# Seven block products for the outputs of six systems in the last pass of layer two, and squared Relu as two ScalarE steps

## The chip, the cores and the metric

The kernel runs on one core of one Trainium2 chip (trn2). The metric is device microseconds of one execution. A profiled execution gives busy times per engine and a trace of every instruction: PE is TensorE's matmul, PEld its weight load, DVE VectorE, ACT ScalarE, POOL GpSimd, SP the engine that issues the DMAs. The mean granted clock of TensorE over the span is 1.000, its level of 2.4 GHz.

## What is computed

A retention attention feeds two feed-forward layers on 2304 tokens of 512 features. The change lies in the second layer, which is, cut to what matters:

```python
def _moe2_ref(x, w_in, w_out):       # x [2304, 512], w_in [512, 2048], w_out [2048, 512]
    h = x @ w_in
    r = np.maximum(h, 0.0)
    g = r * r                        # squared Relu
    return (g @ w_out).astype(np.float32)
```

All values are float32. The kernel multiplies in a fast float32 form (F32R). Each operand is split into a high part and a low part (`hi`, and `lo` = value minus `hi`), and a product is the three matmuls hi by hi, hi by lo and lo by hi.

## The kernel before

Layer two runs in three passes `(2, 0)`, `(2, 1)`, `(2, 2)` of 768 tokens, each of two halves "a" and "b" of 384. A pass has eight **systems** `k` = 0 to 7. A system is 256 of the 2048 hidden features for the pass's 768 tokens, and its `x @ w_in` is computed with seven block products where a plain two-by-two block multiplication has eight (a Strassen-Winograd scheme). So a system has seven **slots** (function `slot`), each of six matmuls of 384 columns (function `product`). A slot accumulates in a PSUM bank (names g, v and z in the trace), and ACT and DVE read the bank between slots: slots 1, 6, 7 and 4 follow each other on one bank, and ACT's copy of one slot must be over before the next may write.

Slots 2, 4 and 3 finish the hidden values (`cag` for half "a", `cbg` for "b"). Squared Relu is there one DVE instruction on `max(x, 0) * x`; in slot 4 ACT does the Relu first. Then `hidden` makes the `hi` part with a cast on ACT and the `lo` part with a subtraction on DVE, 768 columns each (`ho_hi`, `ho_lo`).

The output product is function `out2`. After every second system, the pair's 512 hidden features are multiplied by 512 rows of `w_out`, in six tiles of 128 tokens by 512 features. A tile is twelve matmuls of 512 columns in one of three PSUM banks (`oacc`), and DVE adds it into `xy` (ACT copies it there for the first pair). `xy` holds the layer's input and takes its output. The very last tile is done in two halves of 256 columns. The operands of `w_out` lie split in DRAM (`wsp`), those of `w_in` as sums and splits in `win`; SP loads both a system ahead (`wi`, `wo`).

The program is not run in the order in which it is written: a scheduler takes the code's order as priority and puts an instruction in its engine's queue when its inputs are expected to be there. Each engine then works through its queue in order. So what stands behind what on an engine is fixed when the kernel is built, and a tile of a pool is written again only when its last reader is through. The dictionary `outs` says in which system's loop the tiles of a pair are written out in code, and the loop over `n` at the end writes, for each system, its slots, its loads and those tiles.

Of the kernel before, what the change touches and what calls it, by code (L numbers as in the profile page):

```python
# [12 lines left out]
U32 = mybir.dt.uint32  # L13
# [42 lines left out]

TINY = float(np.uint32(0x38000000).view(np.float32))
# [4 lines left out]
def retention_moe_kernel(  # L62
# [19 lines left out]
    raw_p = pool(ctx, "raw_p", 2)  # L82
    cv_p = pool(ctx, "cv_p", 3)
    mid = ExitStack()
    ctx.enter_context(mid)
    cv2_p = pool(mid, "cv2_p", HOLD - 2)
# [291 lines left out]
    s1_p = pool(ctx, "s1_p", 1, side="right")  # L378
    xs_p = pool(ctx, "xs_p", 4, side="right")
    xo_p = pool(ctx, "xo_p", 1, side="right")  # L380

# [231 lines left out]
    c4_p = pool(ctx, "c4_p", 1, side="right")  # L613
# [34 lines left out]

    def slot(n, i):
# [5 lines left out]
        if i == 1:  # L655
# [9 lines left out]
        relu2 = dict(scalar=0.0, op0=ALU.max, op1=ALU.mult)  # L665
# [10 lines left out]
        elif i == 2:  # L676
            tt(out=a[:, 0], in0=s["z"], in1=a[:, 0], op=ALU.add)
            if what == "g":
                act.activation(out=a[:, 0], in_=a[:, 0], **silu)
            elif what == "v":  # L680
                tt(out=ga[:, 0], in0=a[:, 0], in1=ga[:, 0], op=ALU.mult)
            else:
                dve.scalar_tensor_tensor(out=a[:, 0], in0=a[:, 0], in1=a[:, 0], **relu2)
        elif i == 4:
            if what == "g":
                act.activation(out=a[:, 1], in_=x, **silu)
            elif what == "v":
                tt(out=ga[:, 1], in0=x, in1=ga[:, 1], op=ALU.mult)
                hidden(n, "a", ga)
            else:  # L690
                act.activation(out=a[:, 1], in_=x, func=AF.Relu)
                dve.scalar_tensor_tensor(out=a[:, 1], in0=x, in1=a[:, 1], **relu2)
                hidden(n, "a", a)
        elif i == 3:
# [7 lines left out]
            else:  # L702
                dve.scalar_tensor_tensor(out=b, in0=b, in1=b, **relu2)
# [5 lines left out]
    def hidden(n, which, c):  # L709
        kw = dict(bufs=2) if n > flip - 1 and which == "a" else {}  # L710
# [51 lines left out]
    def out2(n, which, j):  # L762
# [3 lines left out]
        final = n == len(systems) - 1 and which == "b" and j == 2  # L766
        for at in (slice(0, 256), slice(256, 512)) if final else (slice(0, 512),):
            o = out_bank()[:, at]
            for r in range(4):
                w = wos[2 * k - 2 + r]  # L770
                h = [x[:, r % 2, j * P:(j + 1) * P] for x in hid[n - 1 + r // 2, which]]
                three(o, h, (w[:, 0, at], w[:, 1, at]), r == 0, r == 3)
            home = xy[:, at.start // P:at.stop // P, t0:t0 + P]
            src = o.rearrange("p (c q) -> p c q", q=P)
            if k == 1:
                act.copy(home, src)
            else:
                tt(out=home, in0=src, in1=home, op=ALU.add)
            if k == F2 // 2 - 1:
                sp.dma_start(out=out[t0:t0 + P, at].rearrange("p (c q) -> p c q", q=P), in_=home)  # L780

    flip = systems.index((2, 0, 0, "i"))
    outs, fetch = {}, {}
    for n, (ph, p, k, what) in enumerate(systems):
# [6 lines left out]
        if what == "i":  # L791
            fetch.setdefault((n + 1 + (k + p == 0), 0), []).append((n, range(2 * k, 2 * k + 2)))
        if what == "i" and k % 2:
            for x, which in enumerate("ab"):
                outs.setdefault(n + 2 + x, []).extend((out2, n, which, j) for j in range(3))
# [19 lines left out]
    for n in range(end + 4):  # L815
# [24 lines left out]
        for x in fetch.get((n, 0), []):  # L840
            load_out(*x)
        for x in seq:
# [7 lines left out]
            if n == flip + 1 and i == 4:  # L850
# [3 lines left out]
                ho_p = pool(ctx, "ho2_p", 3)  # L854
                wo_p = pool(ctx, "wo2_p", 8)
# [7 lines left out]
            place[:] = place[1:] + [dve.recent]  # L863
            if (ph, p) in PACE:
# [5 lines left out]
        for _ in make:  # L870
            pass
        if (ph, p) == (2, 0) and systems[n + 1][1]:
            for _ in convert:
                pass

# [60 lines left out]
```

## Time and profile before

| what | value |
|---|---|
| three runs | 875.12, 876.67, 877.28 us, median 876.67 us |
| span of the profiled execution | 875.1 us |
| PE, PEld busy | 863.9 us (99%), 746.0 us (85%) |
| DVE, ACT, POOL busy | 642.8 us (73%), 400.9 us (46%), 122.2 us (14%) |
| matmuls | 5064 |
| DMA | 203.62 MB, 233 GB/s over the span |

The profiled execution's span agrees with the lowest of the three runs to a tenth of a microsecond, so next to nothing lies around it; the median is 1.5 us above it. Matmuls overlap in PE's pipeline: the duration of one is longer than the step to the next, so the pace is read from start to start. A row of the timeline that says "x2" holds two instructions.

### The profile page before, as it was taken

Reading aid. Unit: us, or ns where it says so; the run is one execution under the profiler, and the core shown is the slowest. Engines: PE = TensorE matmul, PEld = TensorE weight load, DVE = VectorE, ACT = ScalarE, POOL = GpSimd, SP = SyncE. Lnnn points to the kernel's source line nnn. Section 1 sums busy time; section 2 is a strip of 40 time slices with the busy share of each in tenths; the row PEclk is TensorE's granted clock in tenths of the full one; section 3 lists DMA queues with packets and bytes.
Section 4 is the critical chain, followed back from the end, with each engine's and each line's share of the span. In section 5 each row is a group of like instructions: output and inputs, shape, how many; then the busy total and the mean of one; then the engine's idle time right before and its main releaser. Section 6 shows DMA issues by size and latency. Waiting matters only on the chain.

```text
span 875.1 us, 13516 instructions
## 1 busy us (share of the span) xinstructions
PE 863.9 (99%) x5064; PEld 746.0 (85%) x5064; DVE 642.8 (73%) x1002; ACT 400.9 (46%) x709; POOL 122.2 (14%) x135
## 2 busy tenths in 40 slices
PE   9989999999999999999999999999999999999998
PEld 7878888888888888888888899989899988998987
DVE  3899999998976899677647999999534467533544
ACT  3657777565544544644325466554233233232310
POOL 3343343223130010000002311120000000000000
PEclk9999999999999999999999999999999999999999
DMA  9994777755554489878745388988666465656412
GB/s 337 402 356 160 253 249 249 264 186 211 196 192 154 139 282 379 297 273 288 253 141 185 144 315 328 361 304 313 206 239 215 126 226 210 190 202 204 164 41 73
DMA packets 75218, 203.62 MB, mean 233 GB/s; under 512 B 7696, under 2 KB 18448, under 8 KB 75152
## 3 DMA queue, kind: packets, MB, share of 16 engines
q1 hardware_dynamic: 74720, 202.34, 65.8%
q8 instruction: 40, 0.66, 0.3%
q10 hardware_dynamic: 432, 0.41, 0.1%
q14 instruction: 26, 0.21, 0.1%
HBM read 138.23 MB, written 64.49 MB: 232 GB/s over the span
## 4 chain that ended last, share of the span: by engine, by line
PE 86%; DVE 7%; DMA 4%; issue 2%; ACT 1%; SPq 0%; POOL 0%; DVEq 0%; POOLq 0%; ACTq 0%
PE oacc L113 42%; PE g L113 24%; PE v L113 12%; PE z L113 6%; DVE w L113 3%; DMA qk_sb<-in_qk 3%; DVE wi L113 1%; PE o L113 1%; DMA k_sb<-in_kv 1%; DMA qs_sb<-in_qscale 1%; PE s L113 1%; DVE xy L113 1%; DVE cbg L113 0%; PE kv L113 0%; DVE xo_l L113 0%
## 5 line engine op out<-in xcount | busy, mean ns | idle before, releaser
L113 PE MATMUL g<-xo_h,wi 128*128 128x384 f32 (+1 forms) x768 | 238.3, 364 | 0.0
L113 PE MATMUL oacc<-wo,ho_hi 128*128 128x512 f32 (+1 forms) x584 | 179.5, 388 | 0.0
L113 PEld LDWEIGHTS g<-xo_h,wi 128*128 128x128 f32 x768 | 142.5, 188 | 17.1
L113 PE MATMUL oacc<-ho_hi,wo 128*128 128x512 f32 (+1 forms) x480 | 151.1, 370 | 0.5 <-ACT xy L113 0.5
L113 DVE TENSOR_TENSOR xy<-oacc,xy 128x512 f32<-128x512 f32 (+1 forms) x155 | 99.6, 648 | 59.6 <-PE oacc L113 59.1
L113 PE MATMUL g<-xo_l,wi 128*128 128x384 f32 (+1 forms) x384 | 139.6, 364 | 0.0
L113 PEld LDWEIGHTS oacc<-wo,ho_hi 128*128 128x128 f32 x584 | 108.4, 188 | 19.2
L113 PE MATMUL v<-xo_h,wi 128*128 128x512 f32 (+1 forms) x384 | 123.2, 364 | 0.0
L113 PE MATMUL oacc<-wo,ho_lo 128*128 128x512 f32 (+1 forms) x292 | 113.3, 390 | 0.0
L113 PEld LDWEIGHTS oacc<-ho_hi,wo 128*128 128x128 f32 x480 | 88.1, 188 | 17.6 <-ACT xy L113 1.3
L113 PE MATMUL oacc<-ho_lo,wo 128*128 128x512 f32 (+1 forms) x240 | 89.1, 371 | 0.0
L113 PEld LDWEIGHTS g<-xo_l,wi 128*128 128x128 f32 x384 | 72.1, 188 | 8.4
L113 DVE TENSOR_SCALAR w<-w 128x512 f32<-128x512 f32 (+1 forms) x136 | 64.9, 480 | 18.0 <-ACT w L113 17.0
L113 PEld LDWEIGHTS v<-xo_h,wi 128*128 128x128 f32 x384 | 71.2, 188 | 8.0
L113 DVE TENSOR_TENSOR cbg<-v,cbg 128x384 f32<-128x384 f32 (+1 forms) x72 | 43.1, 598 | 45.8 <-ACT cbg L113 24.3
L113 ACT ACTIVATE cag<-g 128x384 f32<-128x384 f32 (+1 forms) x36 | 19.0, 528 | 125.2 <-PE g L113 125.1
L113 PE MATMUL v<-xo_l,wi 128*128 128x512 f32 (+1 forms) x192 | 69.8, 363 | 0.0
L113 PEld LDWEIGHTS oacc<-wo,ho_lo 128*128 128x128 f32 x292 | 54.8, 188 | 11.2
L113 PE MATMUL z<-xo_h,wi 128*128 128x512 f32 (+1 forms) x192 | 62.5, 365 | 0.0
L113 ACT CAST ho_hi<-cbg 128x768 fp32r<-128x768 f32 (+1 forms) x36 | 32.7, 908 | 45.5 <-DVE cbg L113 44.4
L113 DVE SCALAR_TENSOR_TENSOR w<-raw,w 128x512 uint32<-128x512 uint32 x68 | 52.5, 773 | 0.7
L113 PEld LDWEIGHTS oacc<-ho_lo,wo 128*128 128x128 f32 x240 | 45.1, 188 | 8.7
(90 smaller groups left out, 1295.6 us busy)
## 6 DMA issues: line engine op xcount, KB each, us to landing
wi<-win SPq DMA_DIRECT2D x84, 512.0 KB, 4.2
raw<-in_w SPq DMA_DIRECT2D x68, 512.0 KB, 4.9
win<-wi SPq DMA_DIRECT2D x60, 512.0 KB, 3.6
wo<-wsp SPq DMA_DIRECT2D x44, 512.0 KB, 6.4
wsp<-wo SPq DMA_DIRECT2D x28, 512.0 KB, 5.2
qk_sb<-in_qk SPq DMA_DIRECT2D x15, 576.0 KB, 7.4
wst<-w SPq DMA_DIRECT2D x32, 256.0 KB, 6.0
wi<-win SPq DMA_DIRECT2D x28, 256.0 KB, 5.4
```

What stands on the lines that cost most here:

```text
L113: i = op(*args, **kw)
```

## The change

Three things change in layer two.

**Squared Relu.** Function `square` does it as Relu and then Square, both on ACT, for all 24 systems. DVE's three instructions per system go.

**Seven products for the outputs.** For systems 0 to 5 of the last pass (`turn_over` is its first system, `PAIRED` = 6) the output of a pair and of 128 tokens of each half is a two-by-two block product with seven products: block rows are 128 tokens of "a" and 128 of "b", block columns 256 output features, and the inner blocks are the pair's 256 features by 256. Function `out3` does one product: six matmuls of 256 columns, in one half of a bank. The bank is not started afresh for each: products 6, 7 and 4 go on top of product 1, product 3 on top of 5, and each state of the bank is added into one or two of `xy`'s blocks before the next product is put on top. For the first pair ACT copies four of the seven. The left operands are three blocks and four sums of blocks of the hidden values. GpSimd makes the sums (`sums2`, four instructions for each 128 tokens, in the part of `xy` that earlier passes have already written out), and `prepare` splits blocks and sums: ACT casts 512, 256 and 1024 columns, DVE subtracts as many (`hs_h`, `hs_l`, two buffers in pool `hl_p`). The hidden values lie in tiles of a pair (`caa`, `cab`), in two pools that take turns. Systems 6 and 7 keep the plain product (`whole`, `out4`).

**Operands of `w_out`.** The four sums of blocks are made during pass `(2, 1)` (`operand_sums`: GpSimd sums, ACT casts and DVE subtractions of 256 columns) and stored in DRAM (`tsp`). In the last pass each system's seven operands are loaded one by one (256 KB each, tile `wt`, functions `operands2` and `follow`). A list `stream` holds the 63 products and the six last tiles; `flow` takes 1.5 of them, later 2.2, with each slot, from the 26th slot of the last loop on, and what is left after the last slot.

```diff
+PRODUCTS = (1, 5, 6, 3, 7, 2, 4)
+SUMS = (6, 5, 4, 7)
+PAIRED = 6
+START = 4
+    def square(dst, src):
+        act.activation(out=dst, in_=src, func=AF.Relu)
+        act.activation(out=dst, in_=dst, func=AF.Square)
...
-                dve.scalar_tensor_tensor(out=a[:, 0], in0=a[:, 0], in1=a[:, 0], **relu2)
+                square(a[:, 0], a[:, 0])
...
-                act.activation(out=a[:, 1], in_=x, func=AF.Relu)
-                dve.scalar_tensor_tensor(out=a[:, 1], in0=x, in1=a[:, 1], **relu2)
+                square(a[:, 1], x)
...
-                dve.scalar_tensor_tensor(out=b, in0=b, in1=b, **relu2)
+                square(b, b)
...
     def hidden(n, which, c):
+        if n >= turn_over:
+            return
...
+    def sums2(n, j):
+        a, b = (x[:, :, :, j * P:(j + 1) * P] for x in pairs_of[n])
+        a11, a12, a21, a22 = (x[:, :, f] for x in (a, b) for f in range(2))
+        sums_of[n, j] = s = xy[:, :, 2 * P * j:2 * P * (j + 1)].rearrange("p i (s q) -> p i s q", q=P)
+        for x, y, z, op in ((0, a21, a22, ALU.add), (2, a11, a21, ALU.subtract),
+                            (1, s[:, 0], a11, ALU.subtract), (3, a12, s[:, 1], ALU.subtract)):
+            pool_e.tensor_tensor(out=s[:, x], in0=y, in1=z, op=op)
+    def prepare(n, j):
+        a, b = (x[:, :, :, j * P:(j + 1) * P] for x in pairs_of[n])
+        hi, lo = (hl_p.tile([P, 7, 2, P], F32R, tag=x, name=f"hs_{x}") for x in "hl")
+        halves[n, j] = hi, lo
+        split(hi[:, 0:2], lo[:, 0:2], a.rearrange("p s f q -> p f s q"))
+        split(hi[:, 2], lo[:, 2], b[:, :, 1])
+        split(hi[:, 3:7], lo[:, 3:7], sums_of[n, j])
+    def out3(n, j, at):
+        ph, p, k, what = systems[n]
+        i = PRODUCTS[at]
+        if at < 2:
+            bank_ = (2, 1 + j % 2 * 2)[at == 0]
+            banks[at] = ps_a.tile([P, 512], F32, tag=f"a{bank_}", name="oacc")
+        o = banks[at % 2 if at < 6 else 0]
+        o = o[:, 256:] if i == 2 else o[:, :256]
+        x = (1, 2, 4, 5, 6, 7, 3).index(i)
+        for s in range(2):
+            hi, lo = (z[:, x, s] for z in halves[n, j])
+            th, tl = (moving[n - 1 + s, i][:, y] for y in range(2))
+            for y, (c, d) in enumerate(((hi, th), (hi, tl), (lo, th))):
+                pe.matmul(
+                    o, c, d, start=i in (1, 5, 2) and s + y == 0, stop=s == 1 and y == 2, skip_group_check=True
+                )
+        which, half = {1: (0, 0), 5: (1, 1), 6: (0, 1), 3: (0, 1), 7: (1, 1), 2: (0, 0), 4: (1, 0)}[i]
...
+        if k == 1 and i in (1, 5, 6, 4):
+            act.copy(home, src)
+        else:
+            tt(out=home, in0=src, in1=home, op=ALU.add)
...
+    def ready_halves():
+        while queue and prepared["n"] < flowed["out"] + 2:
+            n, j = queue.pop(0)
+            (whole if n == end - 1 else prepare)(n, j)
+            prepared["n"] += 1
...
+            past = slots["n"] - begin_at
+            flow(min(int(1.5 * past + 0.7 * max(0, past - 28)), 21 * PAIRED // 2))
```

How this moves the queues is shown at three places; in the rows, names carry their buffer numbers.

**TensorE behind its last slots.** Before, when the slots of the last system are through, a tile of twelve matmuls of 512 columns follows another (three banks, here `oacc_8278`, `oacc_8293`):

```order
L113 MATMUL oacc_8264<-wo_7972,ho_lo_8063 128x512
L113 MATMUL oacc_8278<-wo_8089,ho_hi_8170 128x512 x2
L113 MATMUL oacc_8278<-wo_8089,ho_lo_8171 128x512
L113 MATMUL oacc_8278<-wo_8091,ho_hi_8170 128x512 x2
L113 MATMUL oacc_8278<-wo_8091,ho_lo_8171 128x512
L113 MATMUL oacc_8293<-wo_8089,ho_hi_8170 128x512 x2
L113 MATMUL oacc_8293<-wo_8089,ho_lo_8171 128x512
L113 MATMUL oacc_8293<-wo_8091,ho_hi_8170 128x512 x2
L113 MATMUL oacc_8293<-wo_8091,ho_lo_8171 128x512
```

Now there are two stretches of block products with no slot between them. The first holds 14; it begins with the end of the first pair (`oacc_8145`, halves `hs_h_7990`), and then products of the second pair's first block of tokens (`hs_h_8115`, banks `oacc_8255` and `oacc_8274`) and of its second block (`hs_h_8238`, bank `oacc_8364`) take turns:

```order
L122 MATMUL oacc_8145<-wt_7627,hs_h_7990 128x256 x2
L122 MATMUL oacc_8145<-wt_7627,hs_l_7991 128x256
L122 MATMUL oacc_8255<-wt_7913,hs_h_8115 128x256 x2
L122 MATMUL oacc_8255<-wt_7913,hs_l_8116 128x256
L122 MATMUL oacc_8255<-wt_8131,hs_h_8115 128x256 x2
L122 MATMUL oacc_8255<-wt_8131,hs_l_8116 128x256
L122 MATMUL oacc_8274<-wt_7937,hs_h_8115 128x256 x2
L122 MATMUL oacc_8274<-wt_7937,hs_l_8116 128x256
L122 MATMUL oacc_8274<-wt_8131,hs_h_8115 128x256 x2
L122 MATMUL oacc_8274<-wt_8131,hs_l_8116 128x256
L122 MATMUL oacc_8364<-wt_7913,hs_h_8238 128x256 x2
L122 MATMUL oacc_8364<-wt_7913,hs_l_8239 128x256
```

So three banks take turns and a bank comes back after two other products. The second stretch, behind the last slots, holds 19 and has the same form.

**VectorE beside that.** Before, the last splits and sums into `xy` lie between finished tiles:

```order
L113 SCALAR_TENSOR_TENSOR cbg_8095<-cbg_8095 128x2x384
L113 TENSOR_TENSOR ho_lo_8235<-cag_8094,ho_hi_8234 128x768
L113 TENSOR_TENSOR ho_lo_8261<-cbg_8095,ho_hi_8260 128x768
L113 TENSOR_TENSOR xy_78<-oacc_8278,xy_78 128x4x128
L113 TENSOR_TENSOR xy_78<-oacc_8293,xy_78 128x4x128
```

Now the three splits of the second block (`hs_l_8239`) stand between the sums that make the banks free:

```order
L122 TENSOR_TENSOR hs_l_8239<-caa_7753,hs_h_8238 128x512
L122 TENSOR_TENSOR xy_78<-oacc_8255,xy_78 128x2x128
L122 TENSOR_TENSOR hs_l_8239<-cab_7754,hs_h_8238 128x256
L122 TENSOR_TENSOR xy_78<-oacc_8274,xy_78 128x2x128
L122 TENSOR_TENSOR hs_l_8239<-xy_78,hs_h_8238 128x1024
L122 TENSOR_TENSOR xy_78<-oacc_8364,xy_78 128x2x128
```

Each of the two stretches has two such groups of three splits.

**GpSimd in the last pass.** Before, it has nothing to do there. Now it makes the sums, here those of the first pair (`caa_7535`, `cab_7536`), three blocks of 128 tokens one behind the other:

```order
L122 TENSOR_TENSOR xy_78<-cab_7536 128x256
L122 TENSOR_TENSOR xy_78<-caa_7535,cab_7536 128x256
L122 TENSOR_TENSOR xy_78<-cab_7536 128x256
L122 TENSOR_TENSOR xy_78<-caa_7535,cab_7536 128x256
L122 TENSOR_TENSOR xy_78<-cab_7536 128x256
L122 TENSOR_TENSOR xy_78<-caa_7535,cab_7536 128x256
L122 TENSOR_TENSOR xy_78<-xy_78,caa_7535 128x256 x3
L122 TENSOR_TENSOR xy_78<-caa_7535,xy_78 128x256 x3
```

The first block's fourth sum is the tenth of the twelve. Its cast (`hs_h_7822<-xy_78`, 1024 columns) follows on ACT, and the product that needs it stands on TensorE behind 66 matmuls of 384 columns and 12 of 256, counted from the end of the slot that completes the pair's hidden values.

## Rows read from the trace of the kernel before

**Rows 1.** Page, part 1: span; busy us (share of the span) x instructions.

```profile
span 875.1 us, 13516 instructions
PE 863.9 (99%) x5064; PEld 746.0 (85%) x5064; DVE 642.8 (73%) x1002; ACT 400.9 (46%) x709; POOL 122.2 (14%) x135
```

**Rows 2.** Waits of TensorE, whole span: waited for, us in total, times, longest.

```profile
PE s L113 <- DMA qk_sb<-in_qk: 2.6, 2, 2.2
...
PE oacc L113 <- ACT xy L113: 0.9, 3, 0.4
```

**Rows 3.** Busy us (x instructions) in two stretches of the last pass; clock, DMA share, GB/s.

```profile
760.00:820.00 60.00, 60.00 (x302) 54.13 (x301) 25.20 (x37) 17.44 (x30) 0.00 (x0) 1.00 0.58 194
820.00:875.00 55.00, 51.86 (x259) 45.52 (x257) 23.27 (x34) 8.69 (x14) 0.00 (x0) 1.00 0.27 87
```

**Rows 4.** Timeline of the end: start us, us, engine, instruction, idle before it.

```profile
867.92 0.39 PE L113 MATMUL oacc<-wo,ho_lo 128*128 128x512 f32 x1
...
868.60 0.39 PE L113 MATMUL oacc<-wo,ho_lo 128*128 128x512 f32 x1
...
869.06 0.28 PE L113 MATMUL oacc<-wo,ho_lo 128*128 128x256 f32 x1
...
871.58 0.28 PE L113 MATMUL oacc<-wo,ho_lo 128*128 128x256 f32 x1
871.90 0.42 DVE L113 TENSOR_TENSOR xy<-oacc,xy 128x256 f32<-128x256 f32 x1 [1.01 <-PE oacc L113]
```

**Rows 5.** Timeline around a wait of TensorE for the read of a bank.

```profile
134.54 0.36 ACT L113 COPY xy<-oacc 128x256 f32<-128x256 f32 x1
...
134.96 0.97 PE L113 MATMUL oacc<-xs,wb 128*128 128x256 f32 x6 [0.41 <-ACT xy L113]
...
135.77 0.88 PE L113 MATMUL oacc<-xs,wi 128*128 128x256 f32 x6
```

**Rows 6.** Timeline of TensorE, two matmuls of a slot.

```profile
702.57 0.33 PE L113 MATMUL v<-xo_l,wi 128*128 128x384 f32 x1
...
703.09 0.33 PE L113 MATMUL v<-xo_l,wi 128*128 128x384 f32 x1
```

**Rows 7.** Groups by form: busy us, mean ns of one, idle before; splits on ACT and DVE.

```profile
L113 ACT CAST wi<-w 128x512 fp32r<-128x512 f32 x36 | 22.2, 619 | 20.4 <-DVE w L113 8.8 <-POOL w L113 4.3 <-PE v L113 4.1
...
L113 ACT CAST xo_h<-xy 128x1024 fp32r<-128x1024 f32 x14 | 14.5, 1049 | 12.6 <-DVE xy L113 4.1 <-PE g L113 4.1 <-PE z L113 3.5
...
L113 DVE TENSOR_TENSOR wi<-w_in,wi 128x512 fp32r<-128x512 f32 x24 | 17.1, 716 | 2.1 <-ACT wi L113 2.1
...
L113 DVE TENSOR_TENSOR xo_l<-xy,xo_h 128x1024 fp32r<-128x1024 f32 x14 | 18.1, 1296 | 4.9 <-ACT xo_h L113 4.9
```

**Rows 8.** Groups by form: hidden values of layer two on DVE and ACT.

```profile
L113 DVE SCALAR_TENSOR_TENSOR cbg<-cbg 128x768 f32<-128x768 f32 x24 | 23.4, 974 | 0.1
...
L113 ACT CAST ho_hi<-cbg 128x768 fp32r<-128x768 f32 x24 | 20.0, 835 | 34.1 <-DVE cbg L113 33.2 <-PE oacc L113 0.8
...
L113 ACT ACTIVATE cag<-g 128x384 f32<-128x384 f32 x24 | 11.8, 493 | 102.1 <-PE g L113 102.1
...
L113 ACT ACT_TABLE_LOAD x2 | 2.6, 1283 | 2.2 <-issue 2.2
```

**Rows 9.** GpSimd on sums: one tile's min/median/max ns, then two places of its timeline.

```profile
L113 POOL TENSOR_TENSOR w_in<-w_in x16: 737/772/1492, 325.3 to 586.4; 128x256 f32<-128x256 f32 x16
...
453.43 0.74 POOL L113 TENSOR_TENSOR w_in<-s,w_in 128x256 f32<-128x256 f32 x1 [127.04 <-DVE wi L113]
454.25 0.74 POOL L113 TENSOR_TENSOR w_in<-w_in 128x256 f32<-128x256 f32 x1
...
498.11 2.57 POOL L113 TENSOR_TENSOR w_in<-s,w_in 128x256 f32<-128x256 f32 x1
```

**Rows 10.** GpSimd's same sums by form: busy us, mean ns of one, idle before.

```profile
L113 POOL TENSOR_TENSOR w_in<-w_in 128x256 f32<-128x256 f32 x16 | 14.9, 931 | 1.3
```

**Rows 11.** DMA issues: count, KB each, median us to landing.

```profile
wst<-w SPq DMA_DIRECT2D x32, 256.0 KB, 6.0
...
out<-xy SPq DMA_DIRECT2D x17, 256.0 KB, 2.7
```

More of the change, by code (lines that the diff above doesn't have):

```diff
@@ L765, in out2 @@
         t0 = TOKENS[ph, p]["ab".index(which)] + j * P
[L766 removed]
+        o = out_bank()
+        for r in range(4):
+            w = wos[2 * k - 2 + r]
+            h = [x[:, r % 2, j * P:(j + 1) * P] for x in hid[n - 1 + r // 2, which]]
+            three(o, h, (w[:, 0], w[:, 1]), r == 0, r == 3)
+        home = xy[:, :, t0:t0 + P]
+        src = o.rearrange("p (c q) -> p c q", q=P)
+        if k == 1:
+            act.copy(home, src)
+        else:
+            tt(out=home, in0=src, in1=home, op=ALU.add)
@@ new lines, in operand_sums @@
+    def operand_sums(n):
+        sums(n)
+        yield
+        yield
+        for x in range(4):
+            w = cv_p.tile([P, 512], U32, tag="w", name="tw").bitcast(F32R).rearrange("p (y q) -> p y q", y=2)
+            split(w[:, 0], w[:, 1], raw_o[n][x // 2][:, x % 2 * 256:][:, :256])
+            yield
+            soon(2, lambda x=x, w=w: sp.dma_start(out=tsp[systems[n][2]][:, x], in_=w.bitcast(F32)))
+            if x == 3 and systems[n][2] + 1 < PAIRED:
+                fetch_raw(n + 1)
@@ L814, in retention_moe_kernel @@
     end = len(systems)
-    for n in range(end + 4):
+    for n in range(turn_over):
         ph, p, k, what = systems[n] if n < end else (0, None, 0, "")
@@ L863, in retention_moe_kernel @@
             place[:] = place[1:] + [dve.recent]
+            slots["n"] += 1
+            due()
+            next(make2, None)
             if (ph, p) in PACE:
@@ L874, in retention_moe_kernel @@
                 pass
+    due(10 ** 6)
+    stream = [
+        (n, j, at) for n in range(turn_over + 1, turn_over + PAIRED, 2) for j in range(3) for at in range(7)
+    ]
+    stream += [(end - 1, j, at) for j in range(3) for at in "ab"]
+    flowed, queue, prepared = {"n": 0, "out": 0}, [], {"n": 0}
+    def ready_halves():
[3 more added lines that the diff above has]
+            prepared["n"] += 1
@@ new lines, in follow @@
+    def follow(n, j, at):
+        if at in ("a", "b"):
+            out4(n, at, j)
+        else:
+            out3(n, j, at)
+            if j == 2:
+                for m in (n + 2, n + 3):
+                    if m < turn_over + PAIRED:
+                        if at == 0:
+                            coming[m] = operands2(m)
+                            next(coming[m], None)
+                        if at % 2 or at > 3 or m % 3 != turn_over % 3:
+                            next(coming[m], None)
+        if at in (6, "b"):
+            flowed["out"] += 1
+            ready_halves()
```

194 lines of the change are left out of this document (171 added, 23 removed).

## The prediction

> **What bounds the kernel now.** I read the busy times first, then the waits, then the stretches of the last pass. TensorE is busy for 863.9 of 875.1 us, and no other engine passes 73% [rows 1]. The list of its waits ends the question of what limits layer two: all of them belong to the attention and to layer one, the largest 2.6 us, and not one to layer two [rows 2]. In the last pass TensorE fills all of 760 to 820 us while VectorE works 25.2 and ScalarE 17.4 us of the 60, GpSimd nothing, and the DMAs have 58% [rows 3]. So a microsecond of matmuls that goes is a microsecond off the time, as long as nothing else makes TensorE wait; and work taken from VectorE gives nothing by itself.
>
> **The gain.** Per pair of systems, six tiles of twelve matmuls of 512 columns become 3 x 7 products of six matmuls of 256 columns. The pace is read at the very end, where both widths run without a gap. Of 512 columns the third matmul of each row starts 0.68 us after that of the row before (867.92 to 868.60), so 0.2267 us each; of 256 columns seven such steps lie between 869.06 and 871.58, so 2.52 / 21 = 0.120 us each [rows 4]. Three pairs: 216 x 0.2267 = 49.0 us before, 378 x 0.120 = 45.4 us after, **3.6 us less**. The half-width matmul costs more than half (0.120 against 0.113), which is why a saving of an eighth of the columns gives 7%. Nothing can make this larger. All the rest can only take from it.
>
> **Block products on one bank.** A product may be put on a bank only when the sum before has been read. From the start of a product's last matmul VectorE's read begins 0.32 us later (871.58 to 871.90) and takes 0.42 [rows 4]; TensorE starts 0.06 us after a read ends (134.54 + 0.36 to 134.96), and its first six matmuls then take 0.97 instead of 0.88 us, 0.09 more [rows 5]. So the next product on the bank can start 0.80 us after that last matmul, or effectively 0.89. With one other product in between it would be due at 0.12 + 0.72 = 0.84, which would cost a little each time. But the order shows three banks in turn in the long stretches; with two products between it is due at 1.56, and 0.7 us are free. Elsewhere slots (six matmuls, 0.52 us per three, 1.04 us [rows 6]) lie between. I take nothing for the read itself.
>
> **Splits in front of a read.** The slack does not cover everything that stands ahead on VectorE. A split of 1024 columns takes 1049 ns on ScalarE and 1296 ns on VectorE, one of 512 columns 619 and 716 ns [rows 7], one of 256 about 0.4 on each. Counted from the last matmul of the block whose halves buffer is to be reused (0.28 us till it ends, 0.04 to each next engine), the three casts are over at about 2.2 us, and the big subtraction runs to about 3.5. The read queued behind it was due at 2.5 and ends at 3.9, where the bank's next product is due at 3.7: some 0.3 us with the weight load. Two of the four groups in the long stretches stand like that, 0.6 us. In the last group the reads of two banks crowd behind the splits, and I put 0.6 for it.
>
> **First use of a buffer.** There are two buffers of halves, so a block's halves are split only when the block two before is through. Its first product needs the 512-column part: 0.28 + 0.04 + 0.62 + 0.04 + 0.72 + 0.06 = 1.76 us after that last matmul for its third matmul. Where two products lie between, this is due at 0.12 + 1.44 + 0.24 = 1.80, no wait; where one lies between, at 1.08, a wait of 0.7. By the order of the queues, each of the two cases comes twice: **1.4 us**. The long stretches thus cost 0.6 + 0.6 + 1.4 = 2.6 us; the bounds are 0.6 (the two uses are covered) and 5 (the stalls throw the three banks out of step, and all four groups cost like the worst).
>
> **Squared Relu on ScalarE.** A system loses three VectorE instructions (974 ns for the 768 columns, the others near 0.6) and gets Relu and Square of 768 columns at about 835 ns each and three more of 384 at 493 [rows 8], 3.1 us for ScalarE. Its casts grow from 2 x 0.835 to half of 3 x 2.08, 1.4 us more. From 17.4 of 60 us, which is 4.5 us per system of 15.3, this goes to about 9 us in 14.8. VectorE loses 2.1 us, gets 1.7 more of splits and 2.3 more of sums, and goes from 6.4 to about 8.3. Both still idle two fifths of the time, so I cost the swap at nothing; the cover is that hidden values are made a slot or more ahead of their products. If a cast of 1 us stands in front of slot 7's copy, TensorE waits up to 0.7 us for it, once or twice in the stretch with only slots: up to 1.4, value 0. No table is loaded for Square: the queue holds the same two loads as before [rows 8].
>
> **GpSimd's sums.** For the first pair they are a chain that TensorE runs against. From the last slot matmul that completes the hidden values: 0.37 (matmul), 0.6 (VectorE), 0.84 + 0.48 + 0.84 (Relu, a copy between, Square), ten sums to the end of the first block, a cast of 1.05, together 4.2 us and ten sums. TensorE has 66 x 0.173 + 12 x 0.12 = 12.9 us of other matmuls, and the low half is wanted 0.7 us later and ready 1.3 us later. A sum of 256 columns takes 737 ns at best with 0.82 from start to start, has its median at 772 and once took 2.57 us [rows 9]; the mean is 931 [rows 10]. Ten at 0.82 end the chain at 12.4: a wait of 0.1 for the low half. Ten at 1.01 (the mean and the gap of 0.08) give 14.3: a wait of 2.0. The median gives 0.4. Between these I take **0.9**, bounds 0 and 2. Sums of the later pairs have over 15 us.
>
> **Loads.** The seven operands of a system are 256 KB each. At the border of the second and third pair one is reloaded after its last reader, with about 5 us till its next use; a load of 256 KB lands in 2.7 to 6.0 us [rows 11]. Value 0, bound 1.3. The sums and splits in pass `(2, 1)` lie on engines that are half idle, and no wait for them can reach TensorE before the last pass; nothing.
>
> **Sum.** -3.6 + 2.6 + 0.9 = -0.1 us on the profiled 875.1, which the lowest run equals. On the median: **876.6 us**, no change. Of all bounds: -3.6 + 0.6 = -3.0 to -3.6 + 5 + 2 + 1.3 + 1.4 = +6.1.
>
> **The rivals.**
>
> *The gain stays.* The waits come to no more than 1 us, because the stalls of the first use shift TensorE behind VectorE and so pay the others too, and GpSimd is at its best, since VectorE is emptier now. For it: in the last pass no engine but TensorE is near its limit. Against it: 1.4 us of first use follow from the durations alone. It gives 873.1 to 874.0, say 873.5.
>
> *GpSimd is late.* The chain of sums is priced above at ten sums; each 0.1 us per sum is 1 us of waiting. With the other terms at -1.0, it makes the kernel slower by over 2.6 us from 1.16 us a sum on. Rows of 1.5 and 2.6 us show such sums where VectorE was busy [rows 9], against a median of 0.77. At 1.3 us a sum the wait is 4.9 us: 880.6. The Trainium skill ("GPSIMD Engine Reference", Specifications) speaks for this rival: GpSimd shares its SBUF interface with VectorE and contends with VectorE instructions that have two SBUF inputs, as every split here has. By that, sums beside splits would be slow and those beside reads of PSUM not; the spread in the rows fits, but no row of the last pass shows it, since GpSimd is idle there.
>
> *A load or a cast is late.* Loads at 1.3 or ScalarE at 1.4 on top of the forecast: 877.9 to 878.0, within no change or just above.
>
> **How the numbers follow.** A measurement tells about 0.3%, 2.6 us, from no change: below 874.0 is faster, above 879.3 slower. Forecast 0.50, with its own range 874.5 to 879; the gain stays 0.24; GpSimd late 0.18; load or cast late 0.08. Faster: 0.24 and 0.02 of the forecast, 0.26. Slower: 0.17 of GpSimd's, 0.05 of the forecast, 0.02 of the loads, 0.24. Same: 0.50. The range leaves a tenth at each end: 873.3 to 881.0.
>
> **What would show it.** In the profile after, products of 256 columns should run at 0.120 us; another pace breaks the gain. TensorE's waits should name hs_l or hs_h on VectorE and ScalarE at the two first uses (0.7 each), xy on VectorE in the long stretches (0.3 to 0.6), and once hs_h behind GpSimd's xy, ahead of the first pair's second product. If they are missing, the first rival is right; if the last is above 3 us, the second. What would make all of it wrong is a wait that I do not name: slots waiting for their own bank, or layer two's earlier passes, which now load ScalarE more.

## The result and the profile after

The changed kernel takes **882.01 us** (median of four runs, 880.73 to 882.89) against 875.89 (874.72 to 877.28) for the kernel before: a ratio of 1.0074, 95% interval 1.0061 to 1.0087. It is slower by 6 us, where 876.6 was forecast and 881.0 was the upper end.

The first lines of the page of the changed kernel: span, then busy time of each engine with its share of the span. They answer to [rows 1].

```profile
span 878.9 us, 14250 instructions
PE 864.5 (98%) x5226; PEld 753.4 (86%) x5226; DVE 628.3 (71%) x1010; ACT 483.8 (55%) x876; POOL 166.0 (19%) x195
```

TensorE is busy about as long as before (864.5 and 863.9 us). That shows nothing by itself: the half-width products are shorter, but part of them ran at half speed, as will be seen. The list of TensorE's waits (engine, waited for, total, times, longest) is where the kernels differ; [rows 2] had no wait of layer two.

```profile
PE oacc L122 <- DMA wt<-tsp: 2.8, 1, 2.8
...
PE oacc L122 <- DMA wt<-wsp: 1.2, 1, 1.2
...
PE oacc L122 <- DVE xy L122: 0.9, 2, 0.5
PE oacc L122 <- ACT xy L122: 0.8, 3, 0.4
PE oacc L122 <- DVE hs_l L122: 0.5, 2, 0.2
```

The line for ACT xy is layer one's, as before. The other four are new, and all lie in the last pass. In the timeline of TensorE (start, length of the group, tiles, count, and the idle time before with its releaser) they stand here, each with the matmul before it (the second wait for hs_l, at 849.76, is like that at 823.06):

```profile
812.23 0.28 PE L122 MATMUL oacc<-wt,hs_l 128*128 128x256 f32 x1
815.32 0.50 PE L122 MATMUL oacc<-wt,hs_h 128*128 128x256 f32 x2 [2.82 <-DMA wt<-tsp]
...
818.57 0.63 PE L122 MATMUL oacc<-wt,hs_h 128*128 128x256 f32 x2
818.99 0.41 PE L122 MATMUL oacc<-wt,hs_l 128*128 128x256 f32 x1
819.21 0.63 PE L122 MATMUL oacc<-wt,hs_h 128*128 128x256 f32 x2
...
822.35 0.48 PE L122 MATMUL oacc<-wt,hs_h 128*128 128x256 f32 x2
823.06 0.39 PE L122 MATMUL oacc<-wt,hs_l 128*128 128x256 f32 x1 [0.22 <-DVE hs_l L122]
...
842.81 0.28 PE L122 MATMUL oacc<-wt,hs_l 128*128 128x256 f32 x1
844.28 0.50 PE L122 MATMUL oacc<-wt,hs_h 128*128 128x256 f32 x2 [1.20 <-DMA wt<-wsp]
...
851.63 0.28 PE L122 MATMUL oacc<-wt,hs_l 128*128 128x256 f32 x1
852.32 0.48 PE L122 MATMUL oacc<-wt,hs_h 128*128 128x256 f32 x2 [0.41 <-DVE xy L122]
...
860.42 0.28 PE L122 MATMUL oacc<-wt,hs_l 128*128 128x256 f32 x1
861.21 0.50 PE L122 MATMUL oacc<-wo,hs_h 128*128 128x512 f32 x1 [0.52 <-DVE xy L122]
```

The three rows from 818.57 to 819.21 have no wait, and yet three matmuls take 0.64 us there, not the 0.36 of [rows 4]. The windows tell why (window, length, busy of PE, weight loads, DVE, ACT, POOL, then granted clock, DMA share, GB/s): after the stall the granted clock is at the lower of its two levels, 1.2 GHz, for most of 816 to 820, which makes its mean 0.57.

```profile
812.00:816.00 4.00, 1.18 (x10) 0.98 (x9) 1.70 (x4) 0.00 (x0) 2.50 (x4) 1.00 1.02 352
816.00:820.00 4.00, 4.00 (x23) 4.00 (x22) 1.68 (x4) 0.00 (x0) 0.33 (x1) 0.57 0.26 89
820.00:832.00 12.00, 11.78 (x84) 11.49 (x83) 7.73 (x17) 6.76 (x13) 2.89 (x4) 1.00 0.16 44
```

While TensorE stands (812 to 816) the DMAs run at 352 GB/s and are full: the load is not lost, it stands in a queue. SP's queue shows what is ahead of it (start, length, tiles, count):

```profile
802.27 0.86 SPq L122 DMA_DIRECT2D wi<-win  x2
803.68 1.13 SPq L122 DMA_DIRECT2D wo<-wsp  x1
804.90 1.23 SPq L122 DMA_DIRECT2D wi<-win  x1
806.22 0.65 SPq L122 DMA_DIRECT2D wt<-tsp  x1
...
833.54 0.32 SPq L122 DMA_DIRECT2D wo<-wsp  x1
834.41 0.32 SPq L122 DMA_DIRECT2D wt<-tsp  x1
834.83 0.86 SPq L122 DMA_DIRECT2D wo<-wsp  x2
835.91 0.52 SPq L122 DMA_DIRECT2D wt<-wsp  x1
```

The load that TensorE waited for, the first operand reloaded for pair two's second system, was issued at 806.22 behind four loads of 512 KB; two of 256 KB issued at 801.11 and 801.79 had not landed either. The load of wi just ahead of it (804.90, 1.23 us long) had itself stood in SP's queue for TensorE, so 806.22 is when SP came to the reload, and its buffer may have been free earlier. TensorE went on at 815.32, 9.1 us after the issue; that is the longest landing of a block operand between 795 and 850 us:

```profile
DMA to landing us min/median/max: 2.9/6.3/9.1
```

The same at the next border: issued at 835.91 behind three loads of wo, waited for until 844.28, 8.4 us later.

**The sum of the last pass.** For each matmul I take the time to the next start and subtract what its shape takes undisturbed (0.1195, 0.1735, 0.2275 us for 256, 384, 512 columns). From 745 us to the end the excess is 0.81 us before and 10.13 after. The 9.3 more are: 3.07 at 812.23 (the stall, and the first matmul after it at 0.22 instead of 0.12), 1.46 at 842.81 in the same way, 1.4 of half clock (the matmuls between 816.4 and 819.6 us), 1.13 for the two first uses (hs_l), 1.36 behind reads (xy), and 0.9 in small pieces. Less the 3.6 of gain this is 5.7 us. The kernels' stretches from the start of layer one to the last matmul differ by just that: 79.08 to 871.58 before is 792.50, 77.09 to 875.25 after is 798.16, +5.66. Next to nothing is lost before the last pass. What comes ahead of layer one moves by some 3 us from run to run, so below I give this stretch, called "layers", beside each time; it is that of each kernel's one profiled execution.

One number of the prediction's base was read wrongly. In every run here that has both, the time is 1.8 us more than the span (880.73 and 878.9; 874.73 and 872.9 for a run of the kernel before). The profiled 875.1 thus belongs to some 876.9, and that the lowest run had the same digits looks like chance. It did not move the forecast, which was put on the median.

### The profile page after: what moved, and what is told of

It reads as the page before. It is cut to its first block, busy times and chain, and to the rows that moved or that the text cites. A ratio compares the mean times of both kernels' runs of the same rounds, so it can differ in the third digit from the quotient of the medians.

```text
span 878.9 us, 14250 instructions
## 1 busy us (share of the span) xinstructions
PE 864.5 (98%) x5226; PEld 753.4 (86%) x5226; DVE 628.3 (71%) x1010; ACT 483.8 (55%) x876; POOL 166.0 (19%) x195
## 4 chain that ended last, share of the span: by engine, by line
PE 84%; DVE 7%; DMA 5%; issue 2%; ACT 1%; SPq 0%; POOL 0%; DVEq 0%; ACTq 0%; POOLq 0%
PE oacc L122 40%; PE g L122 24%; PE v L122 12%; PE z L122 6%; DVE w L122 3%; DMA k_sb<-in_kv 2%; DMA wt<-tsp 1%; PE o L122 1%; DVE wi L122 1%; DMA wt<-wsp 1%; DVE xy L122 1%; PE s L122 1%; DMA mask_sb<-in_mask 1%; PE kv L122 1%; DVE cbg L122 0%
## 5 line engine op out<-in xcount | busy, mean ns | idle before, releaser
L122 PE MATMUL g<-xo_h,wi 128*128 128x384 f32 (+1 forms) x768 | 241.5, 364 | 0.0
L122 DVE TENSOR_TENSOR xy<-oacc,xy 128x512 f32<-128x512 f32 (+1 forms) x194 | 112.6, 586 | 71.5 <-PE oacc L122 69.1
L122 PE MATMUL oacc<-wo,ho_hi 128*128 128x512 f32 x384 | 120.3, 392 | 0.0
L122 PEld LDWEIGHTS oacc<-wo,ho_hi 128*128 128x128 f32 x384 | 71.5, 188 | 11.7
L122 PE MATMUL oacc<-wo,ho_lo 128*128 128x512 f32 x192 | 74.1, 393 | 0.0
L122 DVE TENSOR_TENSOR cbg<-v,cbg 128x384 f32<-128x384 f32 (+1 forms) x56 | 34.2, 611 | 41.6 <-PE v L122 26.0
L122 ACT ACTIVATE raw<-raw 128x512 uint32<-128x512 uint16 x68 | 45.8, 673 | 14.2 <-DMA raw<-in_w 14.2
L122 PE MATMUL oacc<-wt,hs_h 128*128 128x256 f32 x252 | 48.1, 290 | 4.4 <-DMA wt<-tsp 2.8
L122 DVE CUSTOM_DVE_ANT_0 w<-raw,w 128x1024 uint16<-128x1024 uint16 x68 | 48.4, 712 | 0.9
```

The lines of the kernel that those rows point to most:

```text
L122: i = op(*args, **kw)
```

## The experiments

**Theory:** operands of the next pair land late, because their buffers come free only one block before their next use and other loads stand ahead of them; the stall and the clock after it are the loss. **Rivals:** ScalarE's extra work delays something; VectorE and ScalarE set the pace of the block products anyway; GpSimd or its neighbours are slow. Ratios are to the kernel before, run on the same chip.

| run | what it is | median us | ratio, 95% interval | layers us |
|---|---|---|---|---|
| before | | 875.2 to 875.9 | 1 | 792.5 |
| after | | 882.01 | 1.0074 (1.0061, 1.0087) | 798.2 |
| e1_square | before + ScalarE's squares | 875.28 | 1.0001 (0.9992, 1.0011) | 792.8 |
| e2_resident | after, 21 loads left out | 876.48 | 1.0008 (0.9999, 1.0017) | 793.5 |
| e3_wo_late | after, wo later | 879.04 | 1.0047 (1.0034, 1.0060) | 795.6 |
| e4_own_home | e3 + a buffer more | 879.65 | 1.0053 (1.0040, 1.0066) | 795.7 |
| e5_wo_last | e4, wo behind all | 877.79 | 1.0023 (1.0014, 1.0032) | 794.5 |
| e6_spread | e5, splits apart | 877.74 | 1.0024 (1.0015, 1.0034) | 794.3 |
| e7_res_spread | e2, splits apart | 877.84 | 1.0029 (1.0019, 1.0038) | 793.8 |
| e8_pool | e6, part on GpSimd | 878.90 | 1.0040 (1.0024, 1.0055) | 795.2 |
| e11_after_mixed | after, written order | 880.85 | 1.0064 (1.0048, 1.0079) | 798.8 |
| e9_mixed | e5, written order | 882.68 | 1.0085 (1.0069, 1.0100) | 798.7 |
| e10_res_mixed | e2, written order | 880.83 | 1.0064 (1.0051, 1.0076) | 797.0 |
| e13_after_mixed_late | after, written order from block 3 | 876.10 | 1.0006 (0.9996, 1.0016) | 792.7 |
| e12_mixed_late | e5, the same | 877.25 | 1.0023 (1.0012, 1.0035) | 793.6 |
| e14_mixed_second | e13, from product 10 | 878.42 | 1.0036 (1.0024, 1.0048) | 793.9 |
| e15_mixed_dve | e13, squares on VectorE | 877.12 | 1.0020 (1.0010, 1.0030) | 793.8 |
| e16_relu_dve | after, squares on VectorE | 877.51 | 1.0021 (1.0013, 1.0030) | 794.0 |

**The second part alone.**

```diff
 (before.py)
+    def square(dst, src):
+        act.activation(out=dst, in_=src, func=AF.Relu)
+        act.activation(out=dst, in_=dst, func=AF.Square)
...
-                dve.scalar_tensor_tensor(out=b, in0=b, in1=b, **relu2)
+                square(b, b)
```

> The kernel before with one part of the change: the squared Relu of layer two in two ScalarE steps. Theory (late operand loads are the loss, the squared Relu costs nothing): 875.9 within 0.9, no wait of TensorE in layer two. Rival (ScalarE's extra 3 us per system delays what TensorE waits for in the three passes of layer two): 877.5 or more, with waits behind ACT xo or hidden values.

1.0001: the squared Relu on ScalarE costs nothing in the kernel before. This rival falls there; for the new last pass see e16 below.

**No reloads.**

```diff
+        if x > 2:
+            for i in PRODUCTS:
+                moving[n, i] = moving[turn_over + x % 2, i]
+            return
```

> The kernel after, but the block products of the second and third pair of systems take the first pair's operands, which stay in SBUF: 28 loads of 256 KB are left out (the output is not the reference's). Theory: the two waits behind wt (3.1 and 1.5 us with the slow matmul behind each) and the stretch at the lower clock (1.4) go, nothing else: 882.0 - 5.9 = 876.1. The waits behind VectorE (xy 1.4, hs_l 1.1) stay. Rival (the casts and reads on VectorE and ScalarE set the pace of the long stretches, and the loads only hid it): the waits return behind hs_l and xy, 880 or more. Second rival (the lower clock comes from the work itself, not from the stall): the low stretch stays, 877.5.

By this edit systems 3, 4 and 5 of the last pass take the operands of systems 1, 0 and 1, and 21 loads are left out, not the 28 of the expectation: system 2 still loads its seven. One of the four wo tiles also gets a buffer of its own.

876.48 against 876.1 expected, and "layers" falls by 4.7 us. No wait behind wt is left; the waits behind VectorE stay, those for hs_l as they were, and xy has four instead of two:

```profile
PE oacc L122 <- DVE xy L122: 1.4, 4, 0.5
```

The two new ones (excess 0.41 us each, at 816.25 and 841.97) stand where the stalls stood, which had covered them, and a slot waits 0.41 us for its own operands at 775 (excess 0.57): that is why 4.7 us come back and not 5.9. There is no low clock in the last pass. So the reloads and what follows them are 4.7 of the 5.7 us.

**What stands ahead of a load.** First the loads of wo, issued after the third pair's operands:

```diff
-        if n == end - 1:
-            load_last(n)
...
+        if (n, j, at) == (turn_over + 5, 0, 1):
+            load_last(end - 1)
...
+            with tc.issue_after(sp.recent):
+                sp.dma_start(out=w.bitcast(F32), in_=wsp[2, "o", f])
```

> The kernel after, with the four 512 KB loads of the last system's output operands (wo) put behind the block operands of the third pair on SP's queue, instead of one between the loads for the second pair and three between those for the third. Theory (the loads land late because others of 512 KB stand in front of them): stall one shrinks by the 1.3 us that 512 KB take, from 3.0 to 1.7, stall two (1.5 us) goes, and the clock may or may not fall: 877.8 to 879.2. Rival (a load is late only because its buffer comes free late, whatever is in front of it): 881 to 882.

879.04, in the expected range, but only one of the theory's two steps came. One 512 KB load fewer ahead of the first reload, and its stall is 1.5 us shorter, without a low clock behind it. Of these 1.5 us only some 0.4 are a shorter landing (8.6 against 9.1 us). The rest is an earlier issue: SP came to this reload at 805.43, which is 728.1 us after the start of layer one, against 729.1 in the kernel after. The second stall is still there: the edit left three wo ahead of the last operand of that pair on SP's queue.

The first two rows are SP's, the others TensorE's:

```profile
802.57 2.77 SPq L122 DMA_DIRECT2D wi<-win  x3
805.43 0.90 SPq L122 DMA_DIRECT2D wt<-tsp  x1
...
814.09 0.51 PE L122 MATMUL oacc<-wt,hs_h 128*128 128x256 f32 x2 [1.27 <-DMA wt<-tsp]
...
844.14 0.50 PE L122 MATMUL oacc<-wt,hs_h 128*128 128x256 f32 x2 [1.12 <-DMA wt<-wsp]
```

Then a buffer of its own for the first four operands of pair two's second system, loaded a block earlier (and pair three's second system into what pair one leaves):

```diff
+            if x == 3 and at < 4:
+                if at % 2:
+                    continue
+                t = u_p.tile([P, 1024], F32, tag=f"u{at // 2}", name="wt")
+            elif x % 3 == 2 and (x == 2 or at > 3):
```

> The kernel after, with wo late as in the run before it, and the first four operands of the second system of pair two in a buffer of their own (those of pair three's second system in the one that pair one left), so that they are loaded a block earlier. Theory: both stalls and the low clock go, 882.0 - 5.9 = 876.1, 875.5 to 877; no wait behind wt over 0.3 us. Rival (VectorE and ScalarE set the pace of the long stretches): waits behind hs_l and xy grow, 880 or more.

The first stall is gone, the second (1.2 us) is still there, a slot waits 0.77 us for its own operands, and the median of 879.65 is above the expectation (the profiled run is its fastest, 877.84). Last, wo behind every operand:

```diff
-            with tc.issue_after(sp.recent):
+            with ExitStack() as st:
+                for x in loaded[-7:]:
+                    st.enter_context(tc.issue_after(x))
```

> The kernel of e4_own_home with the four wo loads behind every block operand of the third pair (in e4 three of them still stood ahead of the last one, and TensorE waited 1.2 us for it). Theory (the order on SP's queue makes the loads late): no wait behind wt is left, and the time is that of e2_resident, 876.5, between 876 and 878. Rival (a reload into a buffer that was just freed is late whatever stands ahead of it): the wait of 1.2 us stays and the time with it, 879 to 880.

877.79: no wait behind wt, with nothing changed from e4 but the place of wo. The rival that a reload into a freed buffer is late whatever stands ahead has fallen. The wait for a slot's own operands has grown to 1.07 us (774.89, wi<-win), and the waits behind VectorE are those of e2_resident. So e5 is still 2.3 us above the kernel before.

**VectorE's order.** Splits handed out one per product, the 1024 columns in two halves:

```diff
-        split(hi[:, 3:7], lo[:, 3:7], sums_of[n, j])
+        parts.extend([ ...
+            lambda: split(hi[:, 3:5], lo[:, 3:5], s[:, 0:2]),
+            lambda: split(hi[:, 5:7], lo[:, 5:7], s[:, 2:4]), ...
...
             out3(n, j, at)
+            if parts:
+                parts.pop(0)()
```

> The kernel of e5_wo_last with the splits of a block handed out one per product, and the one of 1024 columns in two of 512. Theory (in the long stretches a read of a bank stands behind the 1024-column subtraction, 1.2 us on VectorE, and the next product on that bank waits for it): the two waits of 0.4 us behind xy go, that of 0.56 shrinks to 0.1, the first-use waits for hs_l (0.38 each) stay: 1.1 us less than e5_wo_last, 875.4. Rival (those waits come from the sum of VectorE's work, not from its order): no change from e5_wo_last.

> The kernel of e2_resident (operands of the first pair kept for all, 28 loads left out) with the splits handed out as in e6_spread: the same question without any load. Theory: 1.1 us less than e2_resident, 875.4, the two waits of 0.41 us behind xy gone. Rival: 876.5, the waits move to hs_l.

No gain in either (e7_res_spread, at 1.0029 against 1.0008 for e2_resident, is even slower, though its layers are only 0.3 us longer); the theory was wrong. One wait behind xy grew from 0.23 us in e5 to 1.25 in e6, where two splits now ran beside GpSimd's sums for a later block. VectorE first, GpSimd below, e6_spread:

```profile
812.78 1.11 DVE L122 TENSOR_TENSOR hs_l<-xy,hs_h 128x512 fp32r<-128x512 f32 x1
813.81 0.94 DVE L122 TENSOR_TENSOR hs_l<-cab,hs_h 128x256 fp32r<-128x256 f32 x1
```

```profile
812.60 0.74 POOL L122 TENSOR_TENSOR xy<-cab 128x256 f32<-128x256 f32 x1 [2.17 <-DVE hs_l L122]
813.42 1.05 POOL L122 TENSOR_TENSOR xy<-xy,caa 128x256 f32<-128x256 f32 x1
814.44 0.90 POOL L122 TENSOR_TENSOR xy<-caa,cab 128x256 f32<-128x256 f32 x1
```

The splits take 1.11 and 0.94 us, where 512 and 256 columns take 0.69 and 0.42 alone: 0.94 us more, about what the wait grew by. Moving one of them to GpSimd did not help either:

```diff
+    def split_pool(hi, lo, src):
+        act.copy(hi, src)
+        pool_e.tensor_tensor(out=lo, in0=src, in1=f32(hi), op=ALU.subtract)
```

> The kernel of e6_spread with one of the two 512-column subtractions of a block of the second and third pair on GpSimd instead of VectorE. Theory: GpSimd is free there, its 1.5 us end before the products that need them, and VectorE has 0.7 us less ahead of its reads: 0 to 0.5 us less than e6_spread. Rival (GpSimd is too slow, or slows VectorE's splits beside it): waits behind POOL hs_l, 0.5 us or more slower.

878.9, 1.2 us above e6, as the rival's number had it, though the two intervals overlap. No wait names GpSimd. Against e6 the longest wait behind xy shrank (1.25 to 0.55), but there are four of 0.47 to 0.55, a slot's wait for its own operands went from 0.69 to 1.34, and splits of 256 columns beside GpSimd took up to 1.38. So a part of the loss is a load, and not GpSimd.

**Stretches without slots.** In the kernel after, TensorE's queue runs 14 products and more in a row (no slot between 808.9 and 824.36), although the code is written as one or two products, then a slot. The next three hold its queue to the written order, by this and the same for every matmul of a block product:

```diff
+        with ExitStack() as st:
+            if n >= turn_over and flowed["n"]:
+                st.enter_context(tc.issue_after(pe.recent))
             product(n, ...)
```

> The kernel after, with TensorE's queue held to the order in which the code is written: one or two block products, then a slot, all the way, instead of stretches of 14 and 19 products without a slot. Theory (the loads of a pair are late because its buffers come free only 7 products, 5 us, before their next use; with 5 slots between it is 10 us, against a landing of at most 9.1): stall one and stall two go or stay under 1 us together, and with them the low clock; VectorE, which has 4.6 us of work per block of 5.0 us without slots, has half as much per microsecond, and the waits behind xy and hs_l in the first stretch go. 875 to 877.5. Rival (held to that order TensorE waits instead for the slots' operands and for the first use of each pair): 879 or more, the waits behind wi and hs.

> The kernel of e5_wo_last (own buffers, wo last) with TensorE's queue in the written order as in e11_after_mixed. Theory: no wait behind wt, of the waits behind xy and hs_l (2.1 and 1.1 us) only those of the last block stay, 1.3 us: 877.8 - 1.9 = 875.9. If the first stretch's wait for wi (1.2 us at 773) goes too, 874.7. Rival: as for e11, 879 or more.

> The kernel of e2_resident (operands of the first pair for all three, 28 loads left out) with TensorE's queue in the written order. It shows what the written order does where no load can be late. Theory: 876.5 - 1.9 = 874.6. Rival: the waits only move, 876.5 or more.

All three lost, as the rival had it, but nearly all of it in one place: at the start of the flow the held order let a slot stand for its operands (e11_after_mixed, 3.3 us; 5.9 in e9, 3.9 in e10), and the low clock followed. In e11 a block product waited 1.6 us for its split there as well:

```profile
772.10 0.69 PE L122 MATMUL g<-xo_h,wi 128*128 128x384 f32 x1 [3.26 <-DMA wi<-win]
...
779.27 0.38 PE L122 MATMUL oacc<-wt,hs_l 128*128 128x256 f32 x1 [1.55 <-DVE hs_l L122]
```

Behind 780 us there was next to nothing (in e11 two waits behind xy, 0.23 and 0.33 us). So the order was held only from the third block on (`flowed["n"] > 14`), with no other change to the kernel after, and once more with e5's buffers.

> The kernel after with only the order held from the third block on: no buffer added, wo where it was. Theory: with slots between, the reloads of pair two have about 10 us and land in at most 9.1, so no wait behind wt and no low clock; 874 to 875.5. Rival (the reload stays late): a wait behind wt of 1 us or more is left, and 876.5 or more.

> The kernel of e9_mixed, but TensorE's queue is held to the written order only from the third block on; the first two keep the order of the kernel after, in which no slot waits for its operands. Theory (the remaining loss is VectorE's work per microsecond in stretches without slots, and the late loads come from the same stretches): the waits that e9_mixed had at 768 to 776 us are gone, those behind it (0.3, 0.4, 0.5) stay: excess of the last pass 2 to 3 us against the gain of 3.6, so 874 to 875, at or below the kernel before (875.3). Rival (block products cost these waits in any order): 877.8 as e5_wo_last, or more.

e13: 876.10, ratio 1.0006, above the expected 874 to 875.5 but no wait behind wt, and all block operands landed within 6.6 us, although the code of wo and of the buffers is as in the kernel after. "Layers" falls by 5.4 us: all but a little of the loss went with an order. Which order, e13 alone does not tell, for SP's queue moved along with TensorE's: its reloads now go out with single loads of wi between them and ahead of the first wo.

```profile
799.56 0.60 SPq L122 DMA_DIRECT2D wi<-win  x1
800.26 1.18 SPq L122 DMA_DIRECT2D wt<-wsp  x2
801.53 1.05 SPq L122 DMA_DIRECT2D wt<-tsp  x2
...
811.62 0.32 SPq L122 DMA_DIRECT2D wo<-wsp  x1
```

So the theory's 10 us of distance and the shorter queue are not separated here. The waits that are left:

```profile
785.96 0.50 PE L122 MATMUL oacc<-wt,hs_h 128*128 128x256 f32 x2 [0.66 <-ACT xy L122]
...
791.75 0.50 PE L122 MATMUL oacc<-wt,hs_h 128*128 128x256 f32 x2 [0.52 <-DVE xy L122]
...
794.67 0.50 PE L122 MATMUL oacc<-wt,hs_h 128*128 128x256 f32 x2 [0.18 <-ACT xy L122]
...
831.29 0.51 PE L122 MATMUL oacc<-wt,hs_h 128*128 128x256 f32 x2 [0.23 <-DVE xy L122]
...
843.20 0.51 PE L122 MATMUL oacc<-wt,hs_h 128*128 128x256 f32 x2 [0.32 <-DVE xy L122]
```

These five, with the start-up of the matmul around each, are 2.7 of the 3.9 us of excess over the kernel before that eat its gain of 3.6. Three tries at more failed. e12 (e5's buffers, expected 874 to 875) came to 877.25: it has one slot's wait for operands more (0.61 us).

> The kernel of e13_after_mixed_late, with the written order held from the tenth block product on instead of the fifteenth. In e13 three waits of 0.8, 0.7 and 0.3 us fell between 785 and 795 us, where five products still stood together; e9 and e11, held from the start, had none there. Theory (products in a row are what costs): these three shrink to under 0.5 us together, 1.3 us less than e13: 874.8, below the kernel before by 1. Rival (the change from one order to the other costs them wherever it is put): 876.1.

878.42, where 874.8 was expected and the rival had 876.1. The three waits near 790 went, but one slot stood 2.1 us for its bank, behind ScalarE's work on caa.

> The kernel of e13_after_mixed_late with the squared Relu of layer two as before (VectorE squares, ScalarE's Relu for one of three). Theory (two of e13's waits, 0.8 and 0.3 us, are for ScalarE's copies of block products, which stood behind Relu and Square of 768 columns): they go, 0.5 to 1.1 us less than e13: 875.0 to 875.6. Rival (VectorE has less room than ScalarE: its squares now stand ahead of the reads): 876.1 or more, with waits behind DVE xy grown.

> The kernel after with only the squared Relu as before. What the second part of the change is worth inside the new last pass. Theory (in the pass with slots both engines have room, and the losses lie in the stretches without slots, where there is no squaring): 881 to 883, the two waits behind wt stay. Rival (the squares in ScalarE's queue are a part of the loss): 880 or less.

e15 put the squares back to VectorE (the diff of e1, backwards): the waits behind ScalarE shrank, those behind xy on VectorE grew from 1.1 to 2.5 us in all, 1 us slower, as the rival had it. The same edit on the kernel after, e16, gave 877.51, 4.5 us less than the kernel after. That is the number of the rival (880 or less); the theory, by which the two stalls stay, was wrong. The trace shows the way there: SP's queue now has two loads of 512 KB just ahead of the first reload, not four,

```profile
802.59 1.36 SPq L122 DMA_DIRECT2D wi<-win  x2
804.05 0.68 SPq L122 DMA_DIRECT2D wt<-tsp  x1
```

the longest landing is 7.3 us, and one stall of 0.30 is left. So the second part of the change, free by itself, did take part: with it the queues were laid out in the order that stalls. That it was the layout rather than the squares' own time, e13 and e1 bear out: with the squares on ScalarE, e1 loses nothing and e13 does not stall. TensorE still runs 12 and 21 products without a slot in e16, so such stretches alone do not make the loads late; in e5 and e16 the stalls went or shrank with what stands ahead of a reload on SP's queue. Why the layout fell so was not tried.

## Why the prediction was wrong

By its own steps:

- **The gain, -3.6: right.** Products of 256 columns run at 0.120 us wherever nothing waits and the clock is high. By the paces of the sum above (0.1195 and 0.2275) it would be 4.0, so that sum leaves 0.3 us open.
- **Splits in front of a read, 1.2: near in the sum, in part by luck.** It is 1.36 in the trace, but two more (0.41 each) were hidden under the stalls, as e2 shows; without stalls it is 2.1 there.
- **First use of a buffer, 1.4: right in place and number.** Two, both for hs_l, 1.13 together, and in both one product lies between: the block two before ends with the matmul at 821.46 us, and the first use is at 822.35. No other wait names hs_l or hs_h.
- **GpSimd's sums, 0.9: nothing.** The first pair's twelve sums ran from 767.72 to 776.49, and TensorE came to the products that need them at 777.06, after seven slots, without a wait. The rival of a late GpSimd falls: its price per sum, 1.16 us, is far above the mean of the 36 sums, 0.79 us.
- **Squared Relu, 0: right alone (e1)**, and its effect through the order of the queues not foreseen.
- **Loads, 0 with a bound of 1.3: this is the step that failed.** It measured 4.5 us of stalls. The border of the second and third pair was named, and its distance was no worse than the 5 us of the prediction: from issue to the time when the operand was due, 7.0 us (835.91 to 842.93). But the border of the first and second has the same reload (system three takes the homes of system zero), with 6.1 us (806.22 to 812.35), and that was overlooked. And the landing was wrong at both: it was bounded by 6.0 us, and took 8.4 and 9.1. Neither row of [rows 11] is a load: both groups write from SBUF to DRAM, and 2.7 and 6.0 are their medians; in the same trace the longest landing of wst<-w is 8.0 us. What the landing depends on is what stands ahead on SP's queue: 2.9 us at the least, 9.1 behind four loads of 512 KB and two of 256. The prediction does not add up what stands ahead on that queue, whose order could be read.
- **The clock, not named: 1.4 us.** A stall was priced at its length, and the 3.4 us at 1.2 GHz behind the first one were not.

With 4.5 and 1.4 in place of 0, 0 in place of 0.9, 0.9 of small pieces and the two VectorE terms as measured, the sum is -3.6 + 1.4 + 1.1 + 4.5 + 1.4 + 0.9 = +5.7, where the layers moved by 5.66 and the median by 6.1. The sum of bounds (+6.1) only just covered it, and largely by terms that did not come; the range, cut at 881.0, did not, since "a load is late" had 0.08 and its time was set at 1.3 us for one border.

What stays open: why the squares on ScalarE brought the order that stalls, how much of e13 is TensorE's order and how much SP's, and whether a layout exists that keeps the gain. The 0.2 to 0.5 us between e13 and the kernel before are within the noise (interval 0.9996 to 1.0016). No run here beat the kernel before.

## What to carry to other kernels

When a tile is reloaded as soon as its last reader is through, the time that counts is from that reader to the next use, against the landing behind everything that the queue will hold then: list the loads ahead of it, in bytes. A product that becomes shorter also brings the next use nearer. And where a scheduler lays out the queues, a change that is free on its engine can be dear by the order it brings; read the order of the DMA queue as well as the busy times, and where it is bad hold the order, there and not everywhere: held from the start (e11) it cost as much as it saved.

## What the runs showed of the hardware

- **The clock after a pause.** In four of the 18 profiled runs TensorE stood 2.8, 3.3, 3.9 and 5.9 us in the last pass (after, e11, e10, e9), and in each the granted clock went to 1.2 GHz for 3.4 to 6.8 us; in the others the longest pause there was 2.1 us (e14), and the clock stayed at 2.4. In the kernel after, the 2.8 us thus cost 4.5 (3.07 at the stall and 1.4 of half clock).
- **VectorE beside GpSimd.** Splits that ran beside a sum took 0.96 instead of 0.42 us (256 columns) and 1.75 instead of 1.22 (1024); the sums beside them 0.93 and 1.19 instead of 0.74, and two together 2.42. Reads of PSUM beside sums kept their 0.42 (eight of them in this kernel). The kernel after, VectorE and then GpSimd:

```profile
787.45 0.96 DVE L122 TENSOR_TENSOR hs_l<-cab,hs_h 128x256 fp32r<-128x256 f32 x1
788.33 1.75 DVE L122 TENSOR_TENSOR hs_l<-xy,hs_h 128x1024 fp32r<-128x1024 f32 x1
```

```profile
786.93 1.19 POOL L122 TENSOR_TENSOR xy<-cab 128x256 f32<-128x256 f32 x1
788.07 0.93 POOL L122 TENSOR_TENSOR xy<-caa,cab 128x256 f32<-128x256 f32 x1
788.96 2.42 POOL L122 TENSOR_TENSOR xy<-xy,caa 128x256 f32<-128x256 f32 x2
```

  The Trainium skill ("GPSIMD Engine Reference", Specifications) says that GpSimd shares its SBUF interface with VectorE and contends with instructions that have two SBUF inputs. The trace agrees (a split reads two operands in SBUF, a read of a bank one), and shows that the loss is on both sides: 0.5 us for each of these two splits, and 0.2 to 1.0 us in each row of sums.
